# An S5 scan and a linear attention mixed by a gate: smaller first loads, four V matmuls moved forward, a reordered task list, and another issue of the last output

## The chip, the cores and the metric

The kernel runs on one core of a Trainium2 chip. The metric is device time in microseconds (us) of the whole program. Engines are named as in the profile: PE is TensorE (matmuls; PEld is its weight load), DVE is VectorE, ACT is ScalarE, POOL is GpSimd, SP is SyncE, which here only issues DMAs. Each engine runs its own instructions strictly in the order in which the program lists them, and waits on semaphores for the others.

## The reference

The input x is 2048 x 512 in bf16. Two branches and a gate are computed from it:

```python
x = A_x
g = _sigmoid((x * gate_w).sum(-1, keepdims=True))
# a: diagonal complex state space (S5)
Bu = x @ B_bar.T                      # complex, 512 states
h = Lam_bar * h + Bu[:, t, :]         # over 2048 steps
y = 2.0 * (hseq @ Cmat.T).real + x * Dskip
# b: linear attention, 32 heads of 16, features are softmax(p) and softmax(-p)
q, k, v = split(x @ wqkv)
kv = einsum("bhsf,bhsd->bhfd", phi_k, v);  z = phi_k.sum over s
o = (phi_q @ kv) / (phi_q . z + 1e-6)
b = o @ wo
return g * a + (1 - g) * b
```

The output is 2048 x 512 in bf16. (`B_x` is not used.)

## The kernel before

All work is in `_fast_path`. If a value test at its end fails (a flag in `flag_i`), `general_path` computes everything again; with the inputs here it is not entered, but the flag is made, read by every engine and branched on.

**Tiling.** Rows of x are split by their index modulo 4 into four classes f; a class has 512 rows in four tiles a of 128. `xT` holds x transposed (features on partitions). Class 0 is loaded as rows into `xn` by plain DMAs and transposed by TensorE (unit `x_block`, `tr`, line 432), then copied from PSUM to `xT` (line 377 on ScalarE or 379 on VectorE, one helper). Classes 1 to 3 are loaded by `xload` (line 316) with transposing DMAs. `v_unit` (L449) makes V for one tile of 128 rows: four matmuls of 512 columns, one for each 128 rows of the weight `Wv`, whose first half comes by a ScalarE DMA and whose second half comes by an SP DMA (L312). ScalarE copies V to `vx`. The same loads are followed on SP by the transposed B matrices (`BT`, L320), class 3, the small `Wc`, the key and query weights (`WkT`, `WqT`) and `Wo`.

**Stages.** Then follow: the parameters of the scan (`par`, small VectorE and ScalarE steps, begun by a transpose of `vec_n`, L484); the gate's sums (L892); `g_unit` (L676, L681: input of the scan, in four classes each built on the one before); `fold` (L656: key and query weights with the feature map folded in); `k_unit` (L788 key features, exp on ScalarE, sums by VectorE, L819 sums into kv); `scan_unit` (scan over 512 steps on VectorE, results spread by DMAs into `Zs`, L744); `fill_unit` (L756 to L764: the states of the other classes); `q_unit` (L876); `smalls` (L944 to L970: normalisers); and 16 times `mix` (L986 to L1030). A `mix` makes o of a tile, scales it, has SP transpose it (L1010), and adds in one PSUM buffer `py` the scan part (L1002), the skip (L1006) and o times `Wo` (L1019). It is scaled by the gate (`of`: ScalarE L1024 or VectorE L1026) and written out (`od`, L1030) by a DMA on SP or ScalarE. The last tile has two `py` buffers of 256 columns, so that its two halves end one after the other.

**Order.** No scheduler works on the chip. Each piece of work is a task given to `pl.add` with the engines that may do it, an assumed cost, and its dependences. `_Plan.run` goes through the list `ORDER` (L172), a fixed list of numbers: a number shifted right by one is the task's index, and its last bit chooses between two allowed engines. The tasks are emitted in this order, so ORDER alone decides what stands behind what on each engine; costs and due times (`pl.at`) only decide which buffer of a pool a task takes. Memory waits and data waits are then put in as semaphores. Eight semaphores serve all SP and ScalarE DMAs in turn, so a DMA also waits for the one eight places before it.

**The flag.** `fl1` (L1049 to L1052) takes maxima on VectorE, TensorE turns the result into a row (L1054, with `follow=[t_pb]`, so it is planned after the last L1019), `fl2` (L1057, L1058) writes `flag_i`, and `values_load` (L1064) has each engine read it into a register. With `min_val` and `max_val` given, SP runs a bounds check (FUSED_REGOPS, SEQ_ASSERT). SP then waits for every DMA before the program ends.

Of the kernel before, what the change touches and what calls it, by code (L numbers as in the profile page):

```python
# [12 lines left out]
ACT = mybir.ActivationFunctionType  # L13
# [109 lines left out]
def kernel(  # L123
# [43 lines left out]
F = 4  # L167
# [5 lines left out]
    8, 10, 13, 14, 156, 18, 17, 22, 2, 174, 158, 20, 25, 266, 160, 4, 190, 0, 26, 28, 270, 194, 192, 30, 32, 176,  # L173
    268, 34, 93, 38, 36, 40, 132, 162, 42, 182, 178, 274, 44, 46, 79, 196, 67, 758, 272, 83, 166, 184, 71, 60,
    180, 760, 74, 59, 73, 88, 134, 164, 206, 276, 81, 138, 506, 762, 77, 168, 502, 136, 140, 378, 209, 510, 504,
    380, 91, 55, 210, 764, 508, 85, 212, 154, 286, 96, 282, 288, 86, 290, 56, 516, 518, 294, 142, 65, 512, 144,
    292, 285, 6, 148, 528, 515, 522, 146, 53, 766, 521, 296, 330, 524, 336, 304, 530, 444, 48, 527, 150, 152, 332,
    334, 298, 308, 438, 533, 338, 768, 386, 340, 534, 50, 63, 342, 302, 300, 306, 344, 442, 536, 542, 770, 382,
    310, 544, 346, 68, 440, 446, 348, 448, 352, 170, 392, 94, 354, 312, 384, 538, 314, 388, 316, 320, 450, 318,
    540, 470, 452, 356, 322, 324, 394, 476, 546, 362, 326, 328, 454, 358, 397, 350, 172, 100, 360, 404, 98, 478,  # L180
    472, 568, 548, 480, 474, 390, 456, 562, 406, 398, 460, 104, 408, 102, 418, 462, 570, 106, 572, 420, 214, 550,
    564, 422, 482, 400, 552, 484, 464, 466, 108, 486, 220, 222, 600, 554, 488, 110, 402, 566, 364, 410, 574, 556,
    412, 414, 224, 374, 216, 492, 468, 186, 626, 494, 112, 490, 594, 576, 416, 188, 496, 578, 558, 232, 376, 114,
    116, 218, 596, 234, 118, 580, 424, 604, 120, 498, 426, 598, 246, 602, 500, 428, 236, 692, 238, 606, 694, 584,
    226, 630, 248, 696, 430, 228, 628, 122, 586, 632, 230, 686, 588, 608, 640, 124, 642, 250, 718, 688, 458, 240,
    610, 724, 590, 560, 432, 126, 434, 252, 690, 592, 242, 722, 244, 612, 634, 726, 636, 644, 366, 652, 638, 370,
    128, 720, 728, 698, 582, 700, 654, 656, 198, 666, 372, 254, 646, 702, 616, 256, 668, 730, 368, 618, 648, 650,
    670, 704, 786, 200, 732, 436, 258, 734, 614, 278, 708, 658, 280, 660, 774, 710, 834, 620, 790, 792, 788, 662,
    736, 828, 672, 202, 816, 778, 712, 622, 838, 776, 836, 822, 740, 742, 796, 204, 624, 260, 664, 818, 714, 744,
    674, 716, 746, 780, 794, 748, 262, 826, 676, 832, 756, 752, 750, 824, 810, 130, 754, 820, 798, 784, 782, 812,  # L190
    814, 804, 1204, 846, 850, 852, 830, 802, 678, 738, 806, 848, 808, 854, 264, 1222, 840, 1216, 800, 856, 1210,
    948, 1226, 680, 858, 842, 862, 864, 950, 946, 682, 866, 944, 868, 844, 902, 1224, 1212, 1036, 870, 952, 860,
    976, 884, 1214, 954, 978, 996, 1002, 998, 878, 956, 984, 1076, 970, 1004, 1078, 980, 1080, 1048, 960, 972,
    958, 1074, 684, 1022, 974, 1050, 1062, 1006, 1000, 1024, 1054, 1056, 982, 1010, 1052, 1008, 1206, 872, 1028,
    962, 988, 1058, 964, 1060, 1218, 1038, 966, 1030, 968, 1014, 986, 1082, 1026, 1064, 874, 1084, 880, 1208,
    1012, 886, 1132, 1032, 1106, 1108, 1134, 1016, 1066, 1086, 1126, 1034, 882, 1068, 1128, 890, 1100, 1158, 1220,
    990, 1090, 876, 892, 1102, 1070, 1152, 1136, 1160, 1130, 1154, 1110, 1234, 1092, 992, 1138, 1166, 1104, 1094,
    1040, 1042, 894, 1232, 1162, 1184, 1230, 1018, 888, 1112, 1156, 1228, 1178, 1096, 1164, 914, 1186, 1114, 1180,
    1144, 1188, 995, 908, 1168, 1182, 1098, 1044, 1140, 1142, 1170, 1236, 896, 1021, 1118, 904, 1238, 1190, 910,
    1254, 1192, 916, 1256, 1260, 1258, 1240, 898, 1116, 1332, 1244, 1262, 906, 1338, 1120, 912, 1340, 1342, 1306,  # L200
    1334, 1172, 1336, 900, 1246, 1072, 1196, 1312, 1174, 1308, 1264, 1146, 1194, 1314, 1344, 1248, 1122, 1280,
    1198, 1282, 1148, 1177, 1350, 918, 1294, 1266, 1346, 1316, 1250, 1310, 1286, 1272, 1348, 1318, 1296, 920, 938,
    1284, 1252, 1288, 1200, 1290, 1364, 1366, 1352, 1416, 1292, 1358, 926, 1150, 1410, 1268, 922, 1270, 1324,
    1368, 1360, 1418, 932, 928, 1298, 1124, 1412, 1320, 1384, 1274, 924, 1420, 1202, 1414, 1390, 1322, 1362, 930,
    1276, 1422, 934, 1326, 936, 1386, 1278, 1370, 1300, 1436, 1372, 1328, 706, 940, 942, 1424, 1428, 1392, 1442,
    1376, 1438, 1302, 1394, 1444, 1398, 1374, 1388, 1426, 1354, 1331, 1396, 1430, 1046, 1400, 1432, 1440, 1446,
    1448, 1450, 1242, 1402, 1088, 772, 1305, 1435, 1378, 1357, 1380, 1468, 1404, 1454, 1452, 1407, 1409, 1456,
    1458, 1462, 1470, 1472, 1464, 1382, 1466, 1461)
# [5 lines left out]
def _pe(n, cols):  # L214
    return {"PE": n * max(30.0, cols / 2.4 + 3.0)}
# [11 lines left out]
def _fast_path(ctx, tc, A_x, A_Lambda_re, A_Lambda_im, A_B_re, A_B_im, A_C_re, A_C_im, A_log_dt, A_Dskip,  # L227
               B_wqkv, B_w_phi, B_wo, gate_w, out):
    nc = tc.nc
    S, D, H, Dh, Pst = 2048, 512, 32, 16, 512  # L230
    KT, PT, NT, NTI, NG, HG, ZP = 4, 4, 8, 16, 4, 4, 2
    NCH = S // F
    xf = A_x[0].rearrange("(r f) d -> f r d", f=F)
# [15 lines left out]
    flag_i = ctile([1, 1], I32, "flag_i")  # L249
    xT = ctile([P, KT, S], BF16, "xT")  # L250
# [10 lines left out]
    BT = ctile([P, KT, 2, Pst], BF16, "BT")  # L261
# [36 lines left out]
    xn = wk.tile([P, F, D], BF16, tag="ET0", name="xn", bufs=1)  # L298
# [10 lines left out]
    x0 = xf[0].rearrange("(a c) d -> c a d", c=P)  # L309
    nc.sync.dma_start(out=xn[:, 0:2], in_=x0[:, 0:2])  # L310
# [4 lines left out]
    def xload(f):  # L315
        nc.sync.dma_start_transpose(out=xT[:, :, f * NCH:(f + 1) * NCH], in_=xf[f])
    xload(1)
    xload(2)
    for ri, B_ in enumerate((A_B_re, A_B_im)):
        nc.sync.dma_start_transpose(out=BT[:, :, ri, :], in_=B_)  # L320
    for n in range(3):
        nc.scalar.dma_start(out=vec_n[4 * n:4 * n + 4, :], in_=vsrc[n].rearrange("(j p) -> j p", p=P))
    xload(3)
# [24 lines left out]
    pl = _Plan({"DVE": 2.4e3, "ACT": 5.6e3, "PE": 1.1e3, "SP": 27.0e3})  # L348
# [10 lines left out]
    early = {k: pl.held("ET", k) for k in (0, 2, 3)}  # L359
# [23 lines left out]
    d_x = [pl.at(t) for t in (4.1, 6.2, 9.2, 11.4, 19.5)]  # L383
    d_wv0, d_wv, d_b, d_wk, d_wq, d_wo = (pl.at(t) for t in (4.8, 5.6, 17.0, 22.7, 24.8, 27.0))
# [39 lines left out]
    xt = {(a, f): d_x[1 + f] for f in range(1, F) for a in range(4)}  # L424
    dums = []
    pl.unit("x_block")
    for a in range(4):
        b = pl.buf(*A1)

        def tr(e, b=b, a=a):  # L430
            for kt in range(KT):
                nc.tensor.transpose(bfv(b)[:, kt * P:(kt + 1) * P], xn[:, a, kt * P:(kt + 1) * P], ident[:])
        t = pl.add({"PE": 460.0} if a < 2 else _pe(4, 128), tr, deps=[d_x[a // 2]], follow=[t_warm], bufs=[b, early[0]])
        if a < 2:
            dums.append(t)
        xt[a, 0] = evac_task(xT[:, :, tcols(0, a)], b, lambda b: bfv(b).rearrange("p (k c) -> p k c", k=KT), [t],
                             ("ACT", "DVE"), bf=True, rank=9)

    vt = {}

    def v_unit(ti):
        pl.unit("v_unit")
        f, a = ti % F, ti // F
        b = pl.buf(*A1)

        def mm(k0, k1):
            def fn(e):
                for kt in range(k0, k1):
                    MM(out=f32v(b), lhsT=xT[:, kt, tcols(f, a)], rhs=Wv[:, kt, :], start=(kt == 0), stop=(kt == KT - 1))  # L449
            return fn  # L450
        if ti == 0:
            t = pl.add({"PE": 860.0}, mm(0, 2), deps=[xt[a, f], d_wv0], follow=dums, bufs=[b])
            t = pl.add({"PE": 434.0}, mm(2, 4), deps=[d_wv], follow=[t], bufs=[b])
        else:
            t = pl.add(_pe(4, 512), mm(0, 4), deps=[xt[a, f], d_wv], bufs=[b])
        vt[ti] = evac_task(vx[:, ti, :, 0:Dh], b, lambda b: f32v(b).rearrange("p (h e) -> p h e", e=Dh), [t], ("ACT",), rank=8.5)
# [472 lines left out]
    t_pb = None  # L929
# [43 lines left out]
    def mix(f, a, rank=0.0):  # L973
# [22 lines left out]
        yh = []  # L996
# [17 lines left out]
        for n, py in enumerate(pys):  # L1014
# [5 lines left out]
            tb = t_pb = pl.add(_pe(4, w), pb, deps=[t, d_wo], follow=yh[-1:], bufs=[py, oT], rank=rank + 3)  # L1020
# [10 lines left out]
            pl.add({"SP": 600.0, "ACT": 600.0}, od, deps=[to], bufs=[ot], rank=rank + 3, xl={"ACT": 1800.0 + 700.0 * (not last), "SP": 400.0 + 700.0 * (not last)})  # L1031
# [27 lines left out]
    pl.add({"DVE": 400.0}, fl2, deps=[x], bufs=[bf_], rank=20, xl={"DVE": 2300.0})  # L1059
# [4 lines left out]
    return nc.values_load(flag_i[0:1, 0:1], min_val=0, max_val=1)  # L1064
# [620 lines left out]
```

## Time and profile before

| | us |
|---|---|
| median of 4 runs | 151.69 |
| lowest, highest | 151.38, 153.23 |
| the profiled execution | 151.56 |
| its span, first to last instruction | 149.8 |

The profile's page gives the busy time of each engine, the span cut in 40 slices, the DMA queues, the chain of waits that ended last, and the costliest groups of instructions. A busy TensorE is not TensorE at its peak, because matmuls are pipelined and their rows overlap. The DMAs at the start, with the median time from issue to landing:

```profile
xn<-in_A_x_dram SPq DMA_DIRECT2D x2, 256.0 KB, 4.0
Wv<-in_B_wqkv_dram ACTq DMA_DIRECT2D x1, 256.0 KB, 3.9
Wv<-in_B_wqkv_dram SPq DMA_DIRECT2D x1, 256.0 KB, 4.2
xT<-in_A_x_dram SPq DMA_TRANSPOSE x3, 6.1
BT<-in_A_B_re_dram SPq DMA_TRANSPOSE x1, 4.8
```

A name left of the arrow is what is written; "SPq" is the queue of the issuing engine.

### The profile page before, as it was taken

The page shows a single profiled execution, that of the slowest core. Times are in us where ns is not written, and L with a number is a line of the kernel's source. Part 1 is how long each engine was busy: PE and PEld are TensorE (multiplying, and loading weights), DVE is VectorE, ACT ScalarE, POOL GpSimd, SP SyncE. Part 2 cuts the span into 40 slices and gives each one's busy share as a digit, 9 for nine tenths or more (in the row PEclk, how much of TensorE's full clock was granted, in tenths as well). Part 3 has the DMA queues.
Part 4 walks back from the last instruction along what each step waited for, and adds up shares of the span by engine and source line. Part 5 has one row for each costly group of instructions (what it writes and reads, how often), then busy time and mean ns, then how long its engine had stood idle before and what let it go on. Part 6 is the DMA issues. An engine that isn't in the chain of part 4 may idle for free.

```text
span 149.8 us, 3163 instructions
## 1 busy us (share of the span) xinstructions
PE 143.3 (96%) x1124; PEld 82.9 (55%) x1124; DVE 130.5 (87%) x372; ACT 108.9 (73%) x219; POOL 5.3 (4%) x16
## 2 busy tenths in 40 slices
PE   6999999999999999999999999999999999999980
PEld 1444667455566566465546547556646546555550
DVE  2449999889999999999997999999999999999330
ACT  3149988989779799977999989777955566373140
POOL 8600000000000000000000000000000000000000
PEclk9999999999999999999999999999999999999999
DMA  3999999900300032132249963152083127424721
GB/s 108 313 212 237 160 250 218 195 7 0 69 1 0 4 82 97 33 88 92 70 103 123 116 119 99 48 105 38 17 124 73 35 70 107 107 59 116 177 72 48
DMA packets 37260, 14.96 MB, mean 100 GB/s; under 512 B 29432, under 2 KB 37240, under 8 KB 37240
## 3 DMA queue, kind: packets, MB, share of 16 engines
q1 hardware_dynamic: 35488, 13.33, 45.3%
q10 hardware_dynamic: 1592, 1.38, 3.1%
q8 instruction: 10, 0.16, 0.5%
q14 instruction: 10, 0.08, 0.2%
q0 software_dynamic: 160, 0.01, 0.1%
HBM read 1.60 MB, written 2.10 MB: 25 GB/s over the span
## 4 chain that ended last, share of the span: by engine, by line
PE 64%; DVE 21%; DMA 6%; ACT 3%; issue 2%; SPq 0%; DVEq 0%; ACTq 0%
PE pp L676 19%; PE pp L1002 9%; PE pp L788 9%; PE pp L449 9%; PE pp L1019 5%; DMA Zs<-c 4%; DVE late L993 4%; PE pp L681 3%; DVE c L760 3%; DVE c L757 3%; DVE c L756 3%; DMA xn<-in_A_x_dram 2%; PE pp L876 2%; PE pp L819 2%; DVE Gs L764 2%
## 5 line engine op out<-in xcount | busy, mean ns | idle before, releaser
L676 PE MATMUL pp<-xT,BT 128*128 128x512 bf16 x128 | 31.3, 381 | 0.0
L1002 PE MATMUL pp<-CT,Gs 128*128 128x512 bf16 (+1 forms) x104 | 23.7, 363 | 0.1
L676 PEld LDWEIGHTS <-BT 128*128 128x128 bf16 x128 | 17.8, 145 | 8.5
L989 ACT CAST late<-pp 128x512 bf16<-128x512 f32 x32 | 17.8, 593 | 6.4 <-PE pp L986 6.2
L240 ACT ACTIVATE E<-pp 128x512 bf16<-128x512 f32 x32 | 17.4, 615 | 2.3 <-PE pp L819 1.8
L1024 ACT ACTIVATE late<-pp,Gg 128x512 bf16<-128x512 f32 (+1 forms) x16 | 10.5, 668 | 10.1 <-PE pp L1019 7.5
L240 ACT ACTIVATE ET<-pp 128x512 bf16<-128x512 f32 x32 | 17.4, 605 | 0.4 <-PE pp L876 0.3
L1019 PE MATMUL pp<-Wo,late 128*128 128x512 bf16 (+1 forms) x68 | 16.1, 366 | 0.0
L788 PE MATMUL pp<-Wk,xT 128*128 128x512 bf16 x64 | 15.8, 379 | 0.0
L449 PE MATMUL pp<-Wv,xT 128*128 128x512 bf16 x64 | 15.6, 385 | 0.1
L876 PE MATMUL pp<-xT,Wq 128*128 128x512 bf16 x64 | 14.9, 379 | 0.0
L1002 PEld LDWEIGHTS <-Gs 128*128 128x128 bf16 x104 | 9.5, 98 | 8.0 <-DVE Gs L764 0.8
L377 ACT CAST Gs<-pp 128x512 bf16<-128x512 f32 x18 | 10.5, 602 | 2.9 <-PE pp L676 1.5
L993 DVE TENSOR_TENSOR late<-late 128x512 bf16<-128x512 bf16 x32 | 12.5, 417 | 0.0
L986 PE MATMUL pp<-KVbd,ET 128*128 128x128 bf16 x128 | 11.3, 219 | 0.0
L986 PEld LDWEIGHTS <-ET 128*128 128x128 bf16 x128 | 8.7, 97 | 3.6
L377 ACT CAST vx<-pp 128x512 bf16<-128x512 f32 x16 | 8.9, 594 | 2.1 <-PE pp L449 2.1
L788 PEld LDWEIGHTS <-xT 128*128 128x128 bf16 x64 | 6.2, 98 | 7.2
L812 DVE TENSOR_TENSOR E<-E,rc 128x2048 bf16<-128x2048 bf16 x8 | 9.6, 1215 | 0.5 <-ACT rc L240 0.4
L876 PEld LDWEIGHTS <-Wq 128*128 128x128 bf16 x64 | 6.0, 98 | 6.6
L449 PEld LDWEIGHTS <-xT 128*128 128x128 bf16 x64 | 5.9, 98 | 6.6 <-DVE xT L379 0.4
L724 DVE TENSOR_TENSOR_SCAN c<-sp,c 128x512 bf16<-128x512 f32 x8 | 9.3, 1206 | 0.0
(171 smaller groups left out, 242.2 us busy)
## 6 DMA issues: line engine op xcount, KB each, us to landing
Zs<-c SPq DMA_DIRECT2D x32, 64.0 KB, 2.1
c<-c SPq DMA_DIRECT2D x16, 64.0 KB, 2.0
CT<-ET SPq DMA_DIRECT2D x8, 128.0 KB, 5.2
out_dram<-late ACTq DMA_DIRECT2D x8, 128.0 KB, 2.0
out_dram<-late SPq DMA_DIRECT2D x7, 128.0 KB, 2.1
xn<-in_A_x_dram SPq DMA_DIRECT2D x2, 256.0 KB, 4.0
Wo<-in_B_wo_dram SPq DMA_DIRECT2D x4, 128.0 KB, 3.1
Wv<-in_B_wqkv_dram ACTq DMA_DIRECT2D x1, 256.0 KB, 3.9
```

Source lines behind the costliest of these rows:

```text
L240: return nc.scalar.activation(**kw)
L377: nc.scalar.copy(out=o, in_=view(b))
L449: MM(out=f32v(b), lhsT=xT[:, kt, tcols(f, a)], rhs=Wv[:, kt, :], start=(kt == 0), stop=(kt == KT - 1))
L676: MM(out=f32v(b), lhsT=BT[:, kt].rearrange("p r (q t) -> p (r q) t", t=NT)[:, :, j + 4 * h], rhs=xT[:, kt, f * NCH:(f + 1) * NCH], start=( ...
L788: MM(out=f32v(b), lhsT=xT[:, kt, tcols(f, a)], rhs=Wk2[:, kt, :], start=(kt == 0), stop=(kt == KT - 1))
L876: MM(out=f32v(b), lhsT=Wq2[:, kt, g * P:(g + 1) * P], rhs=xT[:, kt, f * NCH:(f + 1) * NCH], start=(kt == 0), stop=(kt == KT - 1))
L986: MM(out=f32v(pn[sgn])[:, g * P:(g + 1) * P], lhsT=ets[f].t[:, sgn, g, cs], rhs=KVbd[:, sgn, g, :], start=True, stop=True)
L989: tn = pl.add(_act(512), lambda e, sgn=sgn: nc.scalar.copy(out=o2.t[:, sgn], in_=f32v(pn[sgn])), deps=[t], bufs=[pn[sgn], o2], rank=rank + 2)
L993: VT(out=v, in0=v, in1=als[f].t[:, a, sgn * H:(sgn + 1) * H].rearrange("p (g h) -> p g h", g=HG).unsqueeze(2).to_broadcast([P, HG, Dh, 8]) ...
L1002: MM(out=f32v(py)[:, 0:w], lhsT=st, rhs=CT[:, tt // 2 + 4 * (tt % 2), n * w:n * w + w], start=(tt == 0), stop=False)
L1019: MM(out=f32v(py)[:, 0:w], lhsT=oT.t[:, g, :], rhs=Wo[:, g, hs], start=False, stop=(g == HG - 1))
L1024: nc.scalar.mul(out=ot.t[:, hs], in_=f32v(py)[:, 0:w], mul=Gg[:, ti:ti + 1])
```

## The change

- The first load of two x tiles becomes two loads of one tile each. The transposing load of class 1 becomes two, of 256 rows each. The imaginary part of B is issued after the vector loads in the program text.
- Tile 4 (the second tile of class 0) gets its V in two tasks along the weight halves, as tile 0 had; the dependence of these on the transposes (`dums`) goes.
- ORDER is a new list of all tasks; one task more than before moves the numbers of all later tasks. With it the copies of `xT` for the third and fourth tile stand on ScalarE, V of tile 4 stands ahead of the transposes of tiles 2 and 3, and the last output half is scaled by VectorE and issued by ScalarE, its first half is issued by SP. Of the 17 output DMAs ScalarE issues 6 instead of 9, SP 11 instead of 8.
- `t_pb` keeps the first half's L1019 task, so the flag's transpose need not follow the second half's. `values_load` loses its bounds.
- Some due times and assumed costs are other numbers.

```diff
-    nc.sync.dma_start(out=xn[:, 0:2], in_=x0[:, 0:2])
+    nc.sync.dma_start(out=xn[:, 0], in_=x0[:, 0])
+    nc.sync.dma_start(out=xn[:, 1], in_=x0[:, 1])
...
-    def xload(f):
-        nc.sync.dma_start_transpose(out=xT[:, :, f * NCH:(f + 1) * NCH], in_=xf[f])
-    xload(1)
+    def xload(f, r0=0, r1=NCH):
+        nc.sync.dma_start_transpose(out=xT[:, :, f * NCH + r0:f * NCH + r1], in_=xf[f][r0:r1])
+    xload(1, 0, NCH // 2)
+    xload(1, NCH // 2, NCH)
     xload(2)
-    for ri, B_ in enumerate((A_B_re, A_B_im)):
-        nc.sync.dma_start_transpose(out=BT[:, :, ri, :], in_=B_)
+    nc.sync.dma_start_transpose(out=BT[:, :, 0, :], in_=A_B_re)
     for n in range(3):
         nc.scalar.dma_start(out=vec_n[4 * n:4 * n + 4, :], in_=vsrc[n].rearrange("(j p) -> j p", p=P))
+    nc.sync.dma_start_transpose(out=BT[:, :, 1, :], in_=A_B_im)
...
-    pl = _Plan({"DVE": 2.4e3, "ACT": 5.6e3, "PE": 1.1e3, "SP": 27.0e3})
+    pl = _Plan({"DVE": 2.4e3, "ACT": 4.4e3, "PE": 1.1e3, "SP": 27.0e3})
...
-    d_x = [pl.at(t) for t in (4.1, 6.2, 9.2, 11.4, 19.5)]
-    d_wv0, d_wv, d_b, d_wk, d_wq, d_wo = (pl.at(t) for t in (4.8, 5.6, 17.0, 22.7, 24.8, 27.0))
+    d_x = [pl.at(t) for t in (4.0, 4.45, 6.3, 8.4, 9.8, 11.5, 19.5)]
+    d_wv0, d_wv, d_b, d_wk, d_wq, d_wo = (pl.at(t) for t in (4.85, 5.7, 17.0, 22.7, 24.8, 27.0))
...
-        if ti == 0:
-            t = pl.add({"PE": 860.0}, mm(0, 2), deps=[xt[a, f], d_wv0], follow=dums, bufs=[b])
+        if ti in (0, 4):
+            t = pl.add({"PE": 434.0}, mm(0, 2), deps=[xt[a, f], d_wv0], bufs=[b])
             t = pl.add({"PE": 434.0}, mm(2, 4), deps=[d_wv], follow=[t], bufs=[b])
...
-            tb = t_pb = pl.add(_pe(4, w), pb, deps=[t, d_wo], follow=yh[-1:], bufs=[py, oT], rank=rank + 3)
+            tb = pl.add(_pe(4, w), pb, deps=[t, d_wo], follow=yh[-1:], bufs=[py, oT], rank=rank + 3)
+
+            t_pb = t_pb if n else tb
...
-    return nc.values_load(flag_i[0:1, 0:1], min_val=0, max_val=1)
+    return nc.values_load(flag_i[0:1, 0:1])
```

The list ORDER begins so before and after (8 is the warm-up task, 10, 14, 18 and 22 are the transposes of x tiles, 156 is the first half of V of tile 0, 174 is V of tile 4 or its first half):

```diff
-    8, 10, 13, 14, 156, 18, 17, 22, 2, 174, 158, 20, 25, 266, 160, 4, 190, 0, 26, 28, 270, 194, 192, 30, 32, 176,
+    8, 10, 13, 14, 156, 17, 0, 174, 176, 18, 22, 20, 24, 2, 4, 178, 158, 192, 268, 162, 26, 272, 30, 28, 194, 760,
```

## The prediction

> **What bounds the kernel now.** I read the page first (shares, slices), then the busy time by stretches, then what TensorE waited for, then both ends in order of time. The page:
>
> ```profile
> PE 143.3 (96%) x1124; PEld 82.9 (55%) x1124; DVE 130.5 (87%) x372; ACT 108.9 (73%) x219; POOL 5.3 (4%) x16
> PE   6999999999999999999999999999999999999980
> ```
>
> TensorE has work in 39 of 40 slices. The table of stretches (busy us of each engine, granted clock, DMA share, GB/s) says where it has not:
>
> ```profile
> 0.00:4.20 4.20, 2.74 (x6) 0.74 (x6) 1.23 (x9) 1.28 (x1) 3.52 (x13) 1.00 0.45 136
> 4.20:7.00 2.80, 2.63 (x19) 1.46 (x20) 1.02 (x4) 0.20 (x1) 1.82 (x4) 1.00 1.18 315
> 7.00:10.00 3.00, 3.00 (x16) 1.24 (x15) 1.41 (x9) 0.97 (x2) 0.00 (x0) 1.00 1.11 239
> 10.00:17.30 7.30, 7.30 (x71) 3.95 (x71) 6.52 (x33) 7.07 (x17) 0.00 (x0) 1.00 1.16 218
> 17.30:95.00 77.70, 77.37 (x622) 46.40 (x621) 74.81 (x191) 70.18 (x144) 0.00 (x0) 1.00 0.47 89
> 95.00:121.00 26.00, 25.92 (x223) 15.04 (x222) 25.67 (x72) 18.09 (x38) 0.00 (x0) 1.00 0.33 62
> 121.00:145.40 24.40, 24.38 (x176) 14.10 (x174) 19.41 (x56) 10.73 (x20) 0.00 (x0) 1.00 0.46 103
> 145.40:149.80 4.40, 0.00 (x0) 0.00 (x0) 0.42 (x2) 0.35 (x1) 0.00 (x0) 0.96 0.16 41
> ```
>
> A busy matmul row can still hide waiting, so I also added up, from start to start, what exceeds a 512-column matmul's usual 0.216 us (the L449 row below: 14 in 3.19 us with the last one's tail) and shorter ones in proportion. From 6.4 to 145.2 us that is only about 1.2 us, of which 0.5 at 94.9 and 0.24 at 120.5; the views of waits name these:
>
> ```profile
> PE pp L1002 <- DVE qmax L956: 0.3, 1, 0.3
> PEld L1002 <- DVE Gs L764: 0.8, 2, 0.5
> ```
>
> So from 6.4 us on TensorE is the bound: work it does earlier comes off the end, and nothing else does. What is open is the first 6.4 us and the last 4.4. The start, TensorE alone:
>
> ```profile
> 3.38 0.63 PE L421 MATMUL pp<-warm 128*128 128x512 bf16 x1
> 4.26 1.03 PE L432 MATMUL pp<-ident,xn 128*128 128x128 bf16 x8 [0.24 <-DMA xn<-in_A_x_dram]
> 5.38 0.96 PE L449 MATMUL pp<-Wv,xT 128*128 128x512 bf16 x2
> 6.36 0.62 PE L432 MATMUL pp<-ident,xn 128*128 128x128 bf16 x8
> 6.82 3.19 PE L449 MATMUL pp<-Wv,xT 128*128 128x512 bf16 x14
> ```
>
> Between 4.26 and 6.82 only 16 transposes and 2 V matmuls run: TensorE waits for x, then VectorE's copy, then the second x pair. The tail: the last matmul ends near 145.4, the flag is written at 145.87, and SP reads it last:
>
> ```profile
> L1064 PEldq TENSOR_LOAD <-flag_i x1: 537/537/537, 145.9 to 145.9; - x1
> L1064 SPq TENSOR_LOAD <-flag_i x1: 522/522/522, 146.2 to 146.2; - x1
> L1064 SPq FUSED_REGOPS  x1: 194/194/194, 146.7 to 146.7; - x1
> L1064 SPq SEQ_ASSERT  x1: 37/37/37, 147.0 to 147.0; - x1
> ```
>
> SP is late because it issues the last output at 145.78 (0.33 us), and then runs two instructions that no other engine has. Its branch comes at 147.07, theirs at 146.50 to 146.55; after it SP walks through all DMA semaphores until 148.9, and the end barrier follows.
>
> **Start of the change.** In the changed program TensorE's order is: transposes of tile 0 and 1, two V matmuls of tile 0, *four* of tile 4 (both weight halves), and only then the transposes of tiles 2 and 3. Estimated from the rows: tile 0 can't be transposed before the warm-ups end (3.81); its 128 KB should land at 3.8 to 4.1, since the loads in flight now land every 0.5 to 0.85 us per 256 KB (4.2, 4.8, 5.5, 6.3). Transposes at the slow clock are 4 x 0.11 a tile: to 4.6, then to 5.0. Tile 0's copy by VectorE (0.43) allows V from 5.1: two at 0.43, to 5.95. Tile 4's four at 0.43 falling to 0.22 end at 6.8, if the second weight half is in by 6.4 (now 5.5; SP issues it one 0.47 us load later). Transposes 2 and 3, 8 x 0.055, end near 7.28. Now they end at 6.82 with 14 V matmuls of the first class to go; then 10. Gain 4 x 0.216 - 0.46 = 0.40 us; bounds 0 (the half weights or the second x pair late by 0.4) and 0.86 (all four fit). Both later copies now stand on ScalarE (0.59 each, till about 8.3); the remaining tile-0 pair and tile 8 (6 x 0.216) cover them.
>
> A rule against this: the Trainium skill, "TensorE: Matmul & The Clock Gate", Part 1, says that the array runs at half rate until a window of about 3.4 us has been busy, on a window that doesn't start with the kernel. The trace: six warm-ups start 0.43 us apart, 14 V matmuls 0.22; the first at the short spacing comes just after 5.8. The granted clock column says 1.00 throughout, so it cannot be read for this. By the rule with a later opening the four added matmuls take 1.72, and the gain of 0.40 becomes a loss of 0.46; by the row it stays. I take the row, as the changed stretch is busier than the present one.
>
> **SP's queue.** One x load more (0.47 us), and the second-class transpose in two commands. No 256-row transpose is in the trace: a 128-row one takes 1.2 us of SP, a 512-row one 1.9 to 2.8; in proportion two halves cost 3.1 against 2.2. So everything behind moves by 0.5 (DMA bandwidth decides; its share is 1.1 to 1.2 there) to 1.4 us (SP decides). What is behind, with its present landing and my estimate of TensorE's need: second half of x 9.8, needed 10.8; third class 10.6, 12.9; both B matrices 15.2, 17.1; fourth class 18.8, 20.5; key weights 21.2, 22.9. Each has 0.9 to 2.2 us of cover, so 0.5 costs nothing and 1.4 costs about 0.4, which with the start gain cancels. I take 0.5. The first half must be there by 9.4; about 8.5 is expected. The B load that now stands behind the vector loads in the text is on SP, they are on ScalarE's queue: order on SP is unchanged. The third vector load waits for the first x tile (about 4.1 instead of 2.25); GpSimd's last one lands at 9.5 and the vector transpose comes at 10.4, so it is hidden.
> On size, "DMA: Bandwidth & Descriptors", Rules for kernel authors, says to coalesce small transfers, and the page's fit for the GpSimd path (Anatomy of one DMA) charges 2.0 us per transfer: two more would be 4 us in series. The four landings above, 0.5 to 0.9 apart for loads issued over 1.5 us, show that these latencies overlap; I charge issue time only.
>
> **The reordered middle.** With each shape's median duration from this trace added in each program's order, VectorE stands 1.4 to 1.6 us further ahead of TensorE from 95 us on (smallest lead of TensorE's work over VectorE's work 10.6 us before, 12.4 after): three dgS scalings and two Gs copies went to ScalarE. ScalarE's lead shrinks by up to 1.7, at 76 to 100 us. Both named waits are for VectorE, so I take 0.2 of their 0.8 as gained; bounds +1.5 (new waits) and -0.7.
>
> SP issues 11 of the 17 outputs instead of 8, each 0.33 to 0.57 us and each waiting for its scaling, with the transposes of o (L1010) queued behind. A transpose needs 0.4 (L995) and 2.4 to land. In the old order the last two stand 7.4 and 7.2 us of TensorE work ahead of their L1019, in the new 3.9 and 4.6: a cover of about 1.1, enough as long as VectorE isn't late (it now ends about 2 us ahead of where it was). Without it TensorE would wait what is missing, up to 1 us.
>
> **Tail.** The flag transpose stays behind *both* halves in TensorE's order: the dependence is loosened, the order doesn't use it. What changes: the second half is scaled by VectorE (256 columns; the 512-column row L1026 takes 0.75, so about 0.48), so the flag's reduction waits until 145.75 instead of 145.42, and the flag comes 0.3 later. SP no longer issues after it: its read starts at 146.2 as now. The two bounds-check instructions go: 146.68 to 147.07, less the 0.05 a plain branch takes, 0.3 us. The last output, on ScalarE at 145.75, lands 1.6 us later as the 64 KB row does (147.4); SP asks for the last semaphore at 147.85, so it is covered by 0.4. Tail: -0.3 (0 if VectorE takes longer, -0.6 if its copy overlaps).
>
> **Sum** against the profiled execution's 151.56 (span 149.8 and 1.76 around it): -0.4 - 0.2 - 0.3 = -0.9, so 150.66; the shown median lies 0.13 above that execution: **150.8**.
>
> **Rivals.**
> Slower: the split transpose costs like two whole ones. Place: SP's queue at 2.7 us; price: 0.47 + 2.2 us, so the second half lands at 12.4, TensorE waits from 10.8 for 1.6 us. Less 0.7 of start and tail: +0.9, 152.6. It decides from a landing after about 11.5. For it: the first whole transpose held SP for 3.8 us. Against: 128-row ones take 1.2. Chance 0.16.
> Slower or even: ScalarE, given 1.7 us more around 76 to 100, becomes the bound there (it is busy 6.75 of 7 us at 88 to 95). Up to 1.5 us of waits, less 0.7: 152.4. Against: VectorE's lead grew. Chance 0.14.
> No change: the start gives nothing (x tile 0 no earlier, slow clock longer) and VectorE's work ahead of the flag eats the tail: 151.6. Chance 0.14.
> More: the start's full 0.86, the waits' 0.7 and 0.4 of tail: -2.0, 149.7. Chance 0.12.
> Forecast: 0.44, own range 150.2 to 151.4.
>
> **How the numbers follow.** This kernel's times spread so that 1% (150.2 to 153.2) is what can be told from no change. Faster: nearly all of the 0.12, and a fifth of the forecast's case: 0.20. Slower: a third of the two slower cases plus what I can't see in 700 reordered tasks: 0.15. Same: 0.65. The range 149.9 to 152.7 leaves out a tenth at each end.
>
> **What would show it.** Right: V matmuls of two tiles before 6.8 us; the first-class V ends by 9.5; no DMA wait at 10 to 17; TensorE's last matmul near 144.8; SP with no FUSED_REGOPS, its branch 0.9 us after the flag is written. Wrong: a TensorE wait for xT near 10.8, an idle stretch of TensorE over 0.5 us after 76 us, or the flag's reduction starting before VectorE's output copy.

## The result, and the profile after

The changed kernel takes 151.08 us (median of 32 runs, 150.26 to 151.96), the kernel before 151.85 (53 runs beside them, 151.38 to 154.08): a ratio of 0.9941, 95% interval 0.9925 to 0.9957. The ratio is over the fast runs and is not that of the two medians, which is 0.9949. The gain is real, and smaller than 1%.

Its profiled execution took 151.45 us with a span of 149.7; the one shown of before took 151.56 with 149.8. This pair shows 0.1 us, where the medians differ by 0.77: the profiled execution of the changed kernel lies 0.37 above its median, that of before 0.29 below its own. The profiles can therefore say which steps of the change happened, and not where all of the 0.77 come from.

The page's shares, and the table of stretches with the borders used for before (busy us of each engine, granted clock, DMA share, GB/s):

```profile
PE 142.7 (95%) x1124; PEld 82.8 (55%) x1124; DVE 129.8 (87%) x368; ACT 110.5 (74%) x223; POOL 5.6 (4%) x16
```

```profile
0.00:4.20 4.20, 2.92 (x10) 1.21 (x10) 1.23 (x9) 1.28 (x1) 3.52 (x13) 1.00 0.50 144
4.20:7.00 2.80, 2.51 (x21) 1.31 (x19) 2.00 (x12) 0.01 (x1) 2.07 (x4) 1.00 1.21 294
7.00:10.00 3.00, 2.98 (x17) 1.20 (x15) 0.00 (x0) 2.14 (x4) 0.00 (x0) 1.00 1.15 222
10.00:17.30 7.30, 7.25 (x83) 3.79 (x81) 5.82 (x29) 5.08 (x12) 0.00 (x0) 1.00 1.34 166
17.30:95.00 77.70, 76.41 (x594) 45.42 (x595) 74.88 (x188) 71.50 (x149) 0.00 (x0) 1.00 0.46 94
...
145.40:149.80 4.40, 0.27 (x3) 0.08 (x1) 0.81 (x3) 0.19 (x1) 0.00 (x0) 0.83 0.27 82
```

Up to 7 us TensorE does 31 matmuls instead of 25, as intended. But the stretch from 17.3 to 95 now holds 1.29 us in which it is idle (77.70 - 76.41), where before it was 0.33. The view of waits names them:

```profile
PE pp L676 <- DMA BT<-in_A_B_im_dram: 0.8, 1, 0.8
PE pp L1002 <- ACT late L989: 0.5, 1, 0.5
```

The first is new: TensorE comes to the first matmuls with B (L676), and the imaginary half of B (the tile BT) isn't there. TensorE alone, from the first x tile to that point, with the wait in brackets:

```profile
3.81 0.63 PE L433 MATMUL pp<-ident,xn 128*128 128x128 bf16 x4
4.65 0.53 PE L433 MATMUL pp<-ident,xn 128*128 128x128 bf16 x4 [0.20 <-DMA xn<-in_A_x_dram]
5.01 1.72 PE L449 MATMUL pp<-Wv,xT 128*128 128x512 bf16 x6
6.57 0.61 PE L433 MATMUL pp<-ident,xn 128*128 128x128 bf16 x8
7.01 3.38 PE L449 MATMUL pp<-Wv,xT 128*128 128x512 bf16 x14
10.33 0.18 PE L484 MATMUL pp<-ident,vec_n 20*128 20x20 bf16 x1
...
18.06 3.65 PE L676 MATMUL pp<-xT,BT 128*128 128x512 bf16 x16 [0.80 <-DMA BT<-in_A_B_im_dram]
```

The same row of before:

```profile
9.94 0.18 PE L484 MATMUL pp<-ident,vec_n 20*128 20x20 bf16 x1
```

The transpose of the vectors (L484) comes at 10.33 us behind 20 V matmuls; before, it came at 9.94 behind 16. Four matmuls of 0.216 less 0.39 of delay is a gain of 0.47 us. Eight us later it is gone. The chain of waits (what released what, followed back from the end; start, duration, what) shows why:

```profile
1.20 3.40 DMA xn<-in_A_x_dram
...
4.62 1.27 SPq L317
...
5.93 2.12 SPq L317
...
8.10 2.69 SPq L321
...
10.84 7.08 DMA BT<-in_A_B_im_dram
...
18.06 3.65 PE pp L676 x16
```

Up to 18 us the path no longer runs over TensorE at all. It runs over SP: the command for the second half of class 1 waits until x tile 1 has landed (4.60), the third class (class 2) and the real half of B follow one after the other, and then comes a load that takes 7.08 us from its command. In the chain of before the same stretch was TensorE's own work, V matmuls above all, and the gate's sums (L892):

```profile
10.38 5.29 PE pp L449 x24
```

Everything that TensorE gains ahead of 17.9 us is worth nothing in this execution.

The tail, in order of time (start, duration, operation):

```profile
145.45 0.22 PE L1056 MATMUL pp<-ident,fb 128*1 128x128 bf16 x1
145.56 0.48 DVE L1028 TENSOR_SCALAR late<-pp,Gg 128x256 bf16<-128x256 f32 x1 [4.75 <-PE pp L1019]
145.96 0.27 DVE L1059 TENSOR_REDUCE ff<-pp 1x1 f32<-1x128 bf16 x1
146.07 0.34 ACTq L1032 DMA_DIRECT2D out_dram<-late  x1
146.26 0.14 DVE L1060 TENSOR_SCALAR flag_i<-ff 1x1 int32<-1x1 f32 x1
```

The group of the line that reads the flag (min/median/max ns, first and last start):

```profile
L1066 SPq TENSOR_LOAD <-flag_i x1: 476/476/476, 146.4 to 146.4; - x1
```

SP reads the flag at 146.43, as the others do, and FUSED_REGOPS and SEQ_ASSERT are gone. From the flag's transpose on TensorE to SP's branch it takes 1.53 us (145.45 to 146.98) instead of 1.91 (145.17 to 147.08), to the end of the program 4.21 instead of 4.60.

The account of the profiled pair, TensorE's time from start to start beyond what its matmuls need: up to 10 us 2.48 instead of 3.06 (-0.58); from 10 to 20 us 1.30 instead of 0.28 (+1.02); from 20 us to the last matmuls 0.16 less, of which the named stalls are 0.06 (at 94.8 us 0.68 instead of 0.50, and the 0.24 at 120.5 gone) and the rest is in small pieces; the tail -0.40. The sum is -0.12, the 0.1 us by which the spans differ. The gain of the start was turned into a new wait.

### The profile page after: what moved, and what is told of

It is laid out like the page before. It is cut to its first block, busy times and chain, and to the rows that moved or that the text cites. A ratio compares the mean times of both kernels' runs of the same rounds, so it can differ in the third digit from the quotient of the medians.

```text
span 149.7 us, 3165 instructions
## 1 busy us (share of the span) xinstructions
PE 142.7 (95%) x1124; PEld 82.8 (55%) x1124; DVE 129.8 (87%) x368; ACT 110.5 (74%) x223; POOL 5.6 (4%) x16
## 4 chain that ended last, share of the span: by engine, by line
PE 79%; DMA 7%; SPq 4%; DVE 4%; ACT 2%; issue 1%; DVEq 0%
PE pp L676 19%; PE pp L1002 17%; PE pp L1019 9%; PE pp L788 9%; PE pp L876 7%; DMA BT<-in_A_B_im_dram 5%; PE pp L986 4%; PE pp L681 3%; PE pp L449 3%; PE pp L819 3%; PE pp L1006 2%; DMA xn<-in_A_x_dram 2%; SPq L317 2%; SPq L321 2%; PE pp L656 1%; DVE KVbd L858 1%
## 5 line engine op out<-in xcount | busy, mean ns | idle before, releaser
L676 PE MATMUL pp<-xT,BT 128*128 128x512 bf16 x128 | 31.7, 380 | 0.8 <-DMA BT<-in_A_B_im_dram 0.8
L676 PEld LDWEIGHTS <-BT 128*128 128x128 bf16 x128 | 17.8, 145 | 10.0 <-issue 1.3
L989 ACT CAST late<-pp 128x512 bf16<-128x512 f32 x32 | 17.5, 589 | 4.8 <-PE pp L986 4.2
L1019 PE MATMUL pp<-Wo,late 128*128 128x512 bf16 (+1 forms) x68 | 16.3, 366 | 0.0
L379 ACT CAST Gs<-pp 128x512 bf16<-128x512 f32 x20 | 11.7, 593 | 1.6 <-PE pp L681 1.2
L986 PE MATMUL pp<-KVbd,ET 128*128 128x128 bf16 x128 | 10.1, 219 | 0.0
L788 PEld LDWEIGHTS <-xT 128*128 128x128 bf16 x64 | 6.0, 97 | 6.3
L449 PEld LDWEIGHTS <-xT 128*128 128x128 bf16 x64 | 5.6, 97 | 6.5 <-DVE xT L381 0.6
```

What stands on the lines that cost most here:

```text
L379: nc.scalar.copy(out=o, in_=view(b))
L676: MM(out=f32v(b), lhsT=BT[:, kt].rearrange("p r (q t) -> p (r q) t", t=NT)[:, :, j + 4 * h], rhs=xT[:, kt, f * NCH:(f + 1) * NCH], start=( ...
L788: MM(out=f32v(b), lhsT=xT[:, kt, tcols(f, a)], rhs=Wk2[:, kt, :], start=(kt == 0), stop=(kt == KT - 1))
L986: MM(out=f32v(pn[sgn])[:, g * P:(g + 1) * P], lhsT=ets[f].t[:, sgn, g, cs], rhs=KVbd[:, sgn, g, :], start=True, stop=True)
L989: tn = pl.add(_act(512), lambda e, sgn=sgn: nc.scalar.copy(out=o2.t[:, sgn], in_=f32v(pn[sgn])), deps=[t], bufs=[pn[sgn], o2], rank=rank + 2)
L1019: MM(out=f32v(py)[:, 0:w], lhsT=oT.t[:, g, :], rhs=Wo[:, g, hs], start=False, stop=(g == HG - 1))
```

## What held up the load of B: the theories

The command of the imaginary half of B goes out at 10.84 us instead of 10.46, and the half lands at 17.92 instead of 15.23. So 0.38 of the 2.7 us come from SP's queue, and 2.3 from the load itself. In the kernel before:

```profile
L320 SPq DMA_TRANSPOSE BT<-in_A_B_im_dram x1: 2217/2217/2217, 10.5 to 10.5; - x1
DMA to landing us min/median/max: 4.8/4.8/4.8
```

On the queue there is a new wait:

```profile
SPq L317 <- DMA xn<-in_A_x_dram: 0.6, 1, 0.6
```

It alone costs nothing yet: the third class is issued at 5.93 us, before at 6.13. But its command then holds SP for 2.12 us (before 1.86) and that of the real half of B for 2.69 (2.39). The DMA view over 14 to 19 us, in 40 slices (busy tenths of the DMA engines, GB/s), for the changed kernel:

```profile
DMA  9999999699990000000000000000049999999999
GB/s 291 293 287 291 271 283 365 162 174 135 39 10 0 0 0 0 0 0 0 0 0 0 0 6 6 10 10 8 10 84 289 289 287 293 289 291 291 293 289 287
q8 instruction: 1, 0.02, 2.6%
```

From 15.4 to 17.6 us next to nothing arrives, and one transfer of a queue with the kind "instruction" begins inside the window (at 14.87 us; it takes 2.08 us for 16 KB). There are ten such transfers over the run, about one for every 225 of TensorE's matmuls and weight loads (1124 of each); they are read here as fetches of TensorE's own instructions. In the kernel before the first one came at 16.65, when the half of B had landed. A second queue of this kind, q14 with 8 KB each, is not what fills the hole: its first transfer comes at 19.05 us, behind it.

First theory: TensorE's instruction fetch stalls the transposing loads, and the new order, which puts three groups of gate matmuls (16 tiny ones each) and the four V matmuls earlier, brings the fetch forward into this load. Second: SP's queue, pushed back by the split load, makes it late. Third: chance, this one execution.

## The experiments

### The changed kernel again

No edit.

> The changed kernel a second time, to see what of its profile recurs. First theory (instruction fetch): the fetch of TensorE's instructions on queue q8 comes again near 14.9 us, inside the load of the imaginary half of B, no packet of which ends for 1 us or more; that half lands 1.5 us or more later than the 15.2 us of before, and TensorE waits for it 0.4 us or more near 18.0. Second theory (SP's queue): the same wait, as the command goes out 0.4 us later each time, but without a hole in the packets. Third theory (chance): the wait is absent or under 0.2 us, and the span is 0.8 us shorter than the first profile's 149.7. Ratio to before 0.992 to 0.996 by all three.

Measured: 151.40 us (12 runs), ratio 0.9949 (0.9925 to 0.9974), span 149.7. The fetch begins at 15.69 us, the half of B lands at 17.91, and TensorE waits for it again:

```profile
PE pp L676 <- DMA BT<-in_A_B_im_dram: 0.6, 1, 0.6
```

```profile
L321 SPq DMA_TRANSPOSE BT<-in_A_B_re_dram x1: 2597/2597/2597, 8.8 to 8.8; - x1
L324 SPq DMA_TRANSPOSE BT<-in_A_B_im_dram x1: 2161/2161/2161, 11.5 to 11.5; - x1
DMA to landing us min/median/max: 5.6/6.0/6.4
```

Chance alone falls. The mixture is another one, though: SP issues the command at 11.48 (1.0 us later than before, as the third class held it for 2.95), and the load takes 6.4 us from there, not 7.1. The three columns of the last row are the two loads' times from command to landing, least, mean of both, greatest.

### Gate groups later

```diff
-    760, 32, 34, 196, 36, 164, 6, 270, 166, 762, 198, 40, 38, 42, 132, 160, 764, 44,
+    760, 32, 34, 196, 36, 164, 6, 270, 166, 198, 40, 38, 42, 132, 160, 44,
...
-    508, 46, 384, 138, 511, 80, 136, 70, 504, 83, 77, 186, 85, 380, 73,
+    508, 46, 384, 762, 138, 511, 80, 136, 70, 504, 83, 77, 186, 85, 380, 764, 73,
```

> The changed kernel with two of the four gate groups (16 one-column matmuls each) moved 15 to 25 tasks later, so that TensorE has 32 matmuls fewer behind it at 14.9 us. First theory (instruction fetch): the fetch on q8 comes at 16 us or later, after the imaginary half of B has landed, which is then at 15.4 to 16.2 us; TensorE needs it from about 17.1 (two gate groups, 0.9 us, less ahead of it) and waits under 0.2 us; the profiled span falls by 0.7 to 1.0 us, the median by 0.3 to 0.9. Second theory (SP's queue): the load still lands near 17.9, TensorE comes to it 0.9 us earlier and waits 1.7 to 1.9 us; the time does not change by more than 0.2. Third theory (chance): no wait, but also none in the repeat of the changed kernel.

Measured: the fetch comes at 19.68 us. In the window from 14 to 19 us no "instruction" transfer of q8 is listed any more, and there is no hole:

```profile
GB/s 279 156 246 293 283 295 291 293 289 218 131 137 195 172 133 127 139 102 150 154 231 289 295 289 287 291 291 291 289 268 92 107 80 98 84 98 150 127 127 115
```

```profile
L320 SPq DMA_TRANSPOSE BT<-in_A_B_re_dram x1: 2467/2467/2467, 9.0 to 9.0; - x1
L323 SPq DMA_TRANSPOSE BT<-in_A_B_im_dram x1: 2167/2167/2167, 11.5 to 11.5; - x1
DMA to landing us min/median/max: 4.8/4.9/5.0
```

The load takes 5.0 us although its command stands as late on SP as in the repeat (11.52). It lands at 16.54, and TensorE starts on B at 16.83 without a wait for it. The hole is now at 19.7 to 21.4 us, in the loads behind. What the first theory forecast for the load came true, but for a landing 0.3 us later than its latest. It overstated the time: the span falls by 0.4 us to 149.3, not by 0.7 to 1.0, as a wait of 0.3 appears ahead of it (V matmuls for a buffer that ScalarE still copies, at 15.97) and the two gate groups have to be done later. The ratio to before is 0.9936 (0.9904 to 0.9968), median 151.30: not to be told from the repeat (151.40). That the wait's absence shortens the kernel is therefore seen in the profiled span, and not in the times.

### The second class of x in one command

Class 1 is loaded whole again:

```diff
-    xload(1, 0, NCH // 2)
-    xload(1, NCH // 2, NCH)
+    xload(1)
```

> The changed kernel with the second class of x loaded by one transposing command again (all else kept), so that SP issues the commands for B 0.3 to 0.5 us earlier. First theory (instruction fetch): the fetch stays at 14.9 give or take 0.5 us; the imaginary half of B lands within 0.5 us of 17.9 (the hole in its packets decides), and TensorE still waits 0.5 us or more there; the time moves by less than 0.3. Second theory (SP's queue): that half lands at 15.3 to 15.7, the wait goes, and the profiled span falls by 0.8 to 1.0. Third theory (chance): no wait, in the repeat as well. Whatever holds, tiles 1 to 2 of the second class have to wait for the whole class (9.75 in the kernel before), which TensorE needs from about 10.8.

Measured: the fetch comes at 14.97 us as expected, the command of the half of B at 10.75. The half lands at 17.11, between the two expectations, and takes 6.4 us from its command, 1.6 more than before (4.8), where the queue adds 0.3. There is no wait for it. TensorE starts on B at 17.87, because in this execution it was slow itself: tile 1 of x landed at 4.73, and its full rate came only at 6.9 us (see below), so that the transpose of the vectors stands at 11.10. The span is 149.4, the ratio 0.9936 (0.9918 to 0.9955), median 151.09, 0.31 under the repeat; the intervals overlap.

How large a part the second theory has depends on the profile that this one is held against. Against the repeat the load is as long (6.4 us), and the half lands 0.8 us earlier because its command goes out 0.7 earlier (10.75, not 11.48). Against the first profile the command is only 0.09 earlier, and the load itself is 0.7 shorter. So the queue has a part in the repeat and next to none in the first profile. In that first profile TensorE would have been ready at 17.26 (18.06 - 0.80), after the 16.54 and 17.11 at which the half lands in the two edited runs. That either delay alone is just covered, and both together make the wait, fits this, but it compares different executions and is not shown.

### The kernel before with 44 small matmuls in the warm-up

```diff
-NWARM = 6
+NWARM = 3
...
             MM(out=bw.t[:], lhsT=warm[:, 0:P], rhs=warm[:], start=True, stop=True)
+        for _ in range(44):
+            MM(out=bw.t[:, 0:1], lhsT=warm[:, 0:P], rhs=warm[:, 0:1], start=True, stop=True)
```

> The kernel before, with 44 one-column matmuls put in the place of three of its six warm-up matmuls, ahead of the first x tile (about 1.4 us for 1.4 us): TensorE has 41 matmuls more behind it at any later time, nothing else is moved. First theory (instruction fetch): the fetch on q8 comes 1.5 to 2.5 us earlier than the 16.6 us of before, inside the load of the imaginary half of B, which lands at 16.5 us or later instead of 15.2; TensorE, which needs it at 17.2, waits 0 to 1.2 us; the time rises by 0 to 1.2 us. Second theory (SP's queue) and third theory (chance): the half of B lands at 15.2 give or take 0.4 and there is no wait. If fewer warm columns cost TensorE its clock, the first matmuls after them are longer, which the rows would show; that would be 0.1 to 0.5 us by itself.

Measured: the fetch moves from 16.65 to 12.70 us, further than expected, and falls into the real half of B, which now takes 6.3 us from its command (4.8 before) and lands at 14.90 instead of 12.86. The imaginary half lands at 16.52. The rows of the two commands:

```profile
L320 SPq DMA_TRANSPOSE BT<-in_A_B_re_dram x1: 2248/2248/2248, 8.6 to 8.6; - x1
L320 SPq DMA_TRANSPOSE BT<-in_A_B_im_dram x1: 3643/3643/3643, 10.8 to 10.8; - x1
DMA to landing us min/median/max: 5.7/6.0/6.3
```

Nothing was reordered and nothing else loaded: matmuls added ahead bring the fetch forward, and the load it meets is late. The run has a second such case: its next fetch, at 27.67 us (31.16 before), falls into the transposing load of C, which takes 6.2 us from its command, not 5.1. No wait came of the late B, since TensorE needed B only at 19.12. The time rose, to 153.06 us (ratio 1.0056, 1.0023 to 1.0089; span 151.6), for the reason that the expectation named last and undersized:

```profile
1.27 1.46 PE L421 MATMUL pp<-warm 128*128 128x512 bf16 x3 [1.27 <-DVE warm L306]
2.53 1.36 PE L423 MATMUL pp<-warm 128*128 128x1 bf16 x44
4.51 1.03 PE L434 MATMUL pp<-ident,xn 128*128 128x128 bf16 x8 [0.63 <-DMA xn<-in_A_x_dram]
...
6.68 1.03 PE L434 MATMUL pp<-ident,xn 128*128 128x128 bf16 x8 [0.43 <-DMA xn<-in_A_x_dram]
7.51 4.45 PE L451 MATMUL pp<-Wv,xT 128*128 128x512 bf16 x14
```

14 V matmuls take 4.45 us here and 3.19 before, and the eight transposes ahead of them 1.03, not 0.62. TensorE has its full rate (0.216 us from one 512-column matmul to the next, not 0.43) only from 10.1 us on. The one-column matmuls, which kept it occupied from 2.5 to 3.9 us, did not stand in for wide ones in this execution; x also came 0.3 us later in it, so the two are not fully apart.

### The start in all six profiles

Times in us; "full rate" is the first start-to-start of 0.22 for 512 columns or 0.055 for 128.

| | vectors' transpose | full rate from | fetch begins | command of B, imaginary | to landing | landed | TensorE on B | span |
|---|---|---|---|---|---|---|---|---|
| before | 9.94 | 6.4 | 16.65 | 10.46 | 4.8 | 15.23 | 17.17 | 149.8 |
| changed | 10.33 | 5.0 | 14.87 | 10.84 | 7.1 | 17.92 | 18.06 | 149.7 |
| changed again | 10.55 | 6.1 | 15.69 | 11.48 | 6.4 | 17.91 | 18.04 | 149.7 |
| gates later | 10.42 | 5.1 | 19.68 | 11.52 | 5.0 | 16.54 | 16.83 | 149.3 |
| x class whole | 11.10 | 6.9 | 14.97 | 10.75 | 6.4 | 17.11 | 17.87 | 149.4 |
| before, small warm-ups | 11.89 | 10.1 | 12.70 | 10.85 | 5.7 | 16.52 | 19.12 | 151.6 |

A half of B with no fetch between its command and its landing took 4.77 to 5.65 us (seven loads), one with a fetch 5.67 to 7.08 (five): the groups touch, but do not overlap. From 94 us on the four executions with the new order run alike: from the stall at 94.4 to 94.8 to the flag's transpose they all take 50.69 us. So their spans differ by what lies ahead of that stall alone.

Not tried: putting V of tile 4 back behind the transposes of tile 2, the bounds check put back, and the flag's transpose moved between the two halves. What is said of them below is read from rows.

## Why the prediction was right, and where it was not

The forecast was 150.8 us against a median of 151.69, a ratio of 0.9941; the measured ratio is the same (0.9949 by the medians). The three terms of its sum were seen about as sized. It left out a wait that costs 0.7 to 1.0 us, which both profiles of the changed kernel have: the profiled pair differs by 0.1 us, not by the forecast 0.9. That the ratio came out is therefore luck in part; if the other executions have as much of the wait, something else, which no profile here shows, makes up for it.

- **Start, -0.40.** Seen: -0.47 in the first profile, with the full rate early in that execution, and -0.25 in the repeat (0.86 less 0.61 of delay). The rule weighed against it (half rate until a window of about 3.4 us has been busy, on a window that doesn't start with the kernel: the Trainium skill, "TensorE: Matmul & The Clock Gate", Part 1) is not refuted, as the prediction had it by choosing the row: the full rate came at 5.0 and at 6.1 us in two executions of the same program, with starts equal to 0.02 us up to 4.1, and at 6.9 in one whose TensorE order is the same. That variation is what a window running by itself would give; the window itself no run here shows. A loss, as the rule would have it (0.46), was seen in the run with the whole x class (0.30: 1.16 of delay less 0.86), not in the changed kernel. The prediction's row puts the first short spacing just after 5.8 us; in before the matmul at 5.79 is followed by a wait for x, and the first two at full rate start at 6.4.
- **SP's queue, 0: the step that failed.** The prediction said "both B matrices 15.2, 17.1", hence "0.9 to 2.2 us of cover, so 0.5 costs nothing". The push was 0.4 and 1.0 us, not far from its bounds of 0.5 to 1.4, and the half-class commands were cheaper than thought (1.33 and 1.27 us, against 1.55 each). It saw that ScalarE's third vector load waits for the first x tile, and missed the like wait of SP's second half. But the landing moved by 2.7 us: the fetch of TensorE's instructions, which had come after the landing (16.65 against 15.23), now fell into the load, which took 7.1 and 6.4 us, not 4.8. The cover of a load was taken from one order of instructions and carried to another.
- **Middle, -0.2.** Seen: -0.16, but only 0.06 of it at the named waits, from which all of it was to come. The two stalls of 0.50 and 0.24 became one of 0.68, and its releaser is ScalarE now (L989), no longer VectorE. This is the second rival in small: 0.2 us instead of up to 1.5.
- **Tail, -0.3.** Seen: -0.38 up to SP's branch in both profiles of the changed kernel (-0.40 to the end), by rows: the second half's scaling takes 0.48 on VectorE as estimated and delays the flag by 0.25; SP's read begins as soon as the flag is written, 0.26 earlier after it than before; the span from SP's read to its branch is 0.55 us, not 0.92, without the two bounds instructions. The sum is -0.38. The change of a few words (flag one group sooner) is not in the order, as said, and no run tried it.
- **Rivals.** A split transpose costing two whole ones: no, 1.3 us each; the second half of the class landed at 9.2. No change: its "start gives nothing" is what the first profile shows at 18 us, by another mechanism than the one named. (The second rival's 152.4 counts from the profiled execution; counted from the median, as the others are, it is 152.5.)
- **Marks.** V of two tiles before 6.8 us, first-class V done by 9.5 (the last of its 16 matmuls starts at 9.15), no FUSED_REGOPS: seen. SP's branch 0.9 us after the flag: 0.58. The last matmul near 144.8: 145.45, which was the sign of the failed step. "No DMA wait at 10 to 17" passed only because the wait stood at 17.3 to 18.1. The idle stretch after 76 us was over 0.5 (0.54 idle, 0.68 from start to start), a "wrong" mark that fired for a cost of 0.2.

Open: why the medians differ by 0.6 to 0.8 us (1.1 at the low end, 151.38 and 150.26) where the profiled pair differs by 0.1. The spans noted for the changed kernel's runs go from 148.5 to 150.2, with the profile's 149.7 near the upper end, and taking the wait away moved the profiled span by 0.2 to 0.4 and the median by 0.1 to 0.3, so part of the other executions may not have it. Before also has a second group of times, which the new order never showed: 9 of its 53 runs took 153.0 to 154.1 us and the others at most 152.3, while no run with the new order, edited or not, took over 152.0. The varying time of the full rate is a candidate for that group (the one profile with a late full rate, 10.1 us, took 153.4), and no run tried it.

## What to carry to other kernels

A landing time read from one profile holds for that order of instructions; before counting on a cover of 1 to 2 us, look for what else used the DMA engines in that stretch, the instruction queue among it, and ask whether the edit moves it. A gain at the start counts only up to the next load that TensorE needs: follow the chain of waits of the changed kernel through that point, not TensorE's row alone. And an early gain that depends on when TensorE comes to its full rate has to be judged from several executions.

## What the runs showed of the hardware

- The profile shows instruction fetches as DMA transfers on queues of their own, ten of 16 KB on q8 in this kernel. In five of the six profiles the first one is followed, 0.1 to 1.1 us after its start, by 0.8 to 2.4 us in which the transposing loads deliver less than 50 GB/s, where they otherwise reach 290; in before it is 0.5 us, 1.5 us after, and a pause as long (at 13.9 us in the repeat) has no fetch ahead of it. A half of B that is hit takes 0.9 to 2.3 us longer than the 4.8 of before, one that is not hit up to 0.9. Moving 32 matmuls back delayed the fetch by 4.0 to 4.8 us, adding 41 ahead brought it forward by 3.95; but between 186 and 244 matmuls and weight loads had run when it came, so their number alone doesn't set its moment. Whether the fetch holds up the loads, or both wait for a third thing, isn't settled; the fetch itself takes 1.0 to 2.1 us.
- The moment of TensorE's full rate differed by 1.1 us between two executions of the same program (5.0 and 6.1), with the granted clock at 1.00 throughout; 44 one-column matmuls in place of three wide ones did not bring it nearer (10.1 us, one execution).
- SP takes 1.3 us for a transposing load of 256 rows and 1.8 to 4.5 for one of 512, by its place in the queue: the third class cost 1.8, 1.9 and 2.1 behind a whole class, and 2.1, 2.95 and 2.97 behind two halves. What the two halves (1.3 each) saved against one whole class (3.8) went into the new wait for x (0.6) and the longer commands behind them.
